# Splitting the blocks that TensorE transposes in the first six attention units: low half from ScalarE instead of VectorE

## The chip, the cores and the metric

The kernel runs on one core of one Trainium2 chip. The core has a matrix engine (PE, TensorE) with its weight loader (PEld), a vector engine (DVE, VectorE), a scalar engine (ACT, ScalarE), a general engine (POOL, GpSimd), an engine that mostly issues transfers (SP, SyncE) and 16 DMA engines. The metric is the device time of one execution in microseconds, the median over runs.

## What is computed

The reference is a block-sparse attention followed by a dense layer pair, in float32:

```python
scores = scale * np.matmul(q, k.transpose(0, 1, 3, 2))    # q, k, v: 4 x 8 x 768 x 64
# mask: neighbouring blocks of 32, first and last block, and 3 sampled blocks for each block row
attn = np.exp(scores - max); attn = attn / (sum + 1e-09); x = np.matmul(attn, v)
h = x @ w_in                                              # 3072 x 512 times 512 x 2048
sp = np.maximum(h, 0.0) + np.log1p(np.exp(-np.abs(h)))
return (h * erf(sp)) @ w_out                              # 2048 x 512
```

The kernel keeps float32 accuracy in products of 16-bit numbers: a float32 matrix is written as a high half (the value rounded to float16) and a low half (what the rounding left), and the products high*high, high*low and low*high are added in PSUM.

## The kernel before

**Units.** For each of the four batches there are 11 "m" units of two inner block rows and four "f" units for the outer block rows. A unit makes scores on PE (`scores`, tile `s`, one buffer), a negated maximum on DVE (`soft_max`, `less`), exponentials on ACT (`soft_exp`, `pf`, two buffers), turns the probabilities so that keys lie on the partitions (`pT`, three buffers), multiplies them with gathered values on PE (`values`, tile `po`, one buffer), divides by the sum on DVE (`norm`, `xf`) and turns the result (`turn`, `xT`). Four units fill one chunk of `xT`.

**Two ways of turning.** From unit 6 on (counted from 0), ACT and DVE first make the high and low half, and a transposing DMA turns both. The first six units (`FIRST = 6`) turn on PE instead, through `by_pe` (line 595): float32 blocks of 128x128 are transposed with an identity matrix `eye` into a PSUM tile `turned` of the pool `ps_h`, ACT takes the high half out of PSUM as float16, and DVE takes out `turned*scale - high` as the low half. `by_pe` runs twice for each of the six units' `pT` (four blocks each time) and once for each of the first four results `xT` (two blocks). The pool `ps_h` has three buffers, and the dense layer's `h` tiles use the same three.

**The weights** are prepared beside the first six units by a generator `weights()`: DVE decodes each pair of weight tiles from 64-bit words (three instructions on 128x1024, `room<-wi` or `room<-wo`), ACT sums squares (`sq_i`, `sq_o`), and the halves are made. For `w_in` PE forms the low half: `rest` is a float32 matmul of the weights with a scaled diagonal, less the high half through `less16` (a negative float16 identity), and ACT takes it out (`wi<-rest`). For `w_out` ACT makes the high half and DVE the low half (`wo<-wo,sums`). Such a float32 matmul appears in the trace as two PE records, a PE transpose as one.

**The dense layers** run in groups: `h` (24 matmuls, `ff_first`), a chain of ACT instructions on `x` and `y` (`ff_logs`, `ff_exp`), the gate on DVE (`ff_gate`, reads `h` and so frees its PSUM buffer), and `o` (12 matmuls, `ff_second`) three groups later.

**Order.** SP and POOL keep the program's order. PE, ACT and DVE keep it only from group 3 on (`held[0] = m >= FF_LAG`, line 989). Everything before that, the six units, the weights and the groups 0 to 2, is ordered by a scheduler that plays the program through with its own cost estimates. Completions of hardware DMAs are counted on eight semaphores (DMAHW0 to DMAHW7) given out in turn, and a DMA that is given one waits until the transfer that had it before has landed.

Of the kernel before, what the change touches and what calls it, by code (L numbers as in the profile page):

```python
# [9 lines left out]
F32 = mybir.dt.float32  # L10
I32 = mybir.dt.int32
BF16 = mybir.dt.bfloat16
AF = mybir.ActivationFunctionType
ALU = mybir.AluOpType
# [4 lines left out]
P = 128  # L19
BLOCK = 32  # L20
P_SHIFT = 14
P_SCALE = 2.0**P_SHIFT
# [9 lines left out]
def sparse_attention_moe(ctx: ExitStack, tc: tile.TileContext, qT, kT, v, sampled, w_in, w_out, out):  # L32
# [7 lines left out]
    class InOrder:  # L40
# [15 lines left out]
    pe, act, dve, pool, sp = (  # L56
        InOrder(e, queued if e in (nc.sync, nc.gpsimd) else held) for e in (nc.tensor, nc.scalar, nc.vector, nc.gpsimd, nc.sync)
    )
# [4 lines left out]
    W = 512  # L63
# [28 lines left out]
    ps_h = ctx.enter_context(tc.tile_pool(name="ps_h", bufs=3, space=PSUM))  # L92
# [6 lines left out]
    room = ld.tile([P, NB, HP, BLOCK], F32, tag="kx", name="room", bufs=2).rearrange("p a b c -> p (a b c)")  # L99
    ones, eye = room[:, :P], room[:, P : 2 * P]  # L100
    less16 = room[:, 2 * P : 2 * P + 64].bitcast(F16)
    diag, line = room[:, 3 * P : 4 * P], room[:, 4 * P : 5 * P]
    column = room[:, 2 * P + 64 : 2 * P + 65]
    mags = [room[:, n : n + 1024].bitcast(I32) for n in (5 * P, 5 * P + 1024)]
    dve.memset(ones, 1.0)
    dve.memset(line[:, :1], 0.0)
# [173 lines left out]
    def indices():  # L280
        room = at.tile([P, 1024], F32, tag="pf", name="ix_room", bufs=2)
        used = 0

        def ix(shape):
            nonlocal used
            n = math.prod(shape[1:])
            part = room[:, used : used + n]
            used += n
            if len(shape) == 3:
                part = part.rearrange("p (a b) -> p a b", b=shape[2])  # L290
            return part

        sf, dd, m1 = ix([P, NB, NR]), ix([P, NB, NR]), ix([P, NB, NR])
        dve.tensor_copy(samp, samp2[:, :, :, 0].rearrange("p i r -> p (i r)"))
        dve.tensor_copy(sf, samp.rearrange("p (i r) -> p i r", r=NR))
        bi = line[:, :NB]
        dve.tensor_tensor(dd, sf, bi.unsqueeze(2).to_broadcast([P, NB, NR]), ALU.subtract)
        dve.tensor_tensor(dd, dd, dd, ALU.mult)
        dve.tensor_scalar(m1, dd, 1.0, None, ALU.is_le)
        dve.scalar_tensor_tensor(dd, sf, -float(NB - 1), sf, ALU.add, ALU.mult)  # L300
        dve.scalar_tensor_tensor(m1, dd, 0.0, m1, ALU.is_equal, ALU.max)
        eq = ix([P, NB, 3])
        for n, (x, y) in enumerate(((1, 0), (2, 0), (2, 1))):
            dve.tensor_tensor(eq[:, :, n], sf[:, :, x], sf[:, :, y], ALU.is_equal)
        dve.tensor_tensor(m1[:, :, 1:], m1[:, :, 1:], eq[:, :, :2], ALU.max)
        dve.tensor_tensor(m1[:, :, 2], m1[:, :, 2], eq[:, :, 2], ALU.max)

        dve.tensor_scalar(eye, line, column, None, ALU.is_equal)
        dve.tensor_scalar(less16, line, column, -1.0, ALU.is_equal, ALU.mult)
        yield  # L310
        dve.tensor_scalar(dd, sf, -1.0, float(NB), ALU.mult, ALU.add)
        dve.tensor_tensor(dd, dd, m1, ALU.mult)
        dve.tensor_tensor(sf, sf, dd, ALU.add)
        pm = turned32[:, :1]
        rows = ix([P, NM])
        dve.memset(rows, 0.0)
        mid = sf[:, 1 : NB - 1]
        for q in range(NR):
            part = slice(q * BLOCK, (q + 1) * BLOCK)
            dve.tensor_scalar(rows[part], mid[part, :, q], float(BLOCK), pm[part], ALU.mult, ALU.add)  # L320
        idx = cp.tile([P, NM], I32, tag="idx", name="idx")
        dve.tensor_copy(idx, rows)
        rows_of.append(idx)
        yield
# [269 lines left out]

    def by_pe(blocks, hi, lo, scale=1.0):
        n = blocks.shape[1]
        turned = ps_h.tile([P, W], F32, tag="h", name="turned")[:, :n]
        for c in range(0, n, P):
            pe.transpose(turned[:, c : c + P], blocks[:, c : c + P], eye)
        turned = turned.rearrange("p (g w) -> p g w", w=hi.shape[2])  # L600
        act.activation(hi, turned, AF.Copy, scale=scale)
        dve.scalar_tensor_tensor(lo, turned, scale, hi, ALU.mult, ALU.subtract)

    def soft_turn(unit):

        s, groups, width, pf = softs.pop(unit)
        pT = at.tile([P, 16, P], F16, tag="pT", name="pT_" + "_".join(str(x) for x in unit), bufs=3)
        parts = pT.rearrange("p (g a k) c -> p g a (k c)", a=2, k=2)
        for n in range(2):
            by_pe(pf[:, n * 512 : (n + 1) * 512], parts[:, 2 * n : 2 * n + 2, 0], parts[:, 2 * n : 2 * n + 2, 1], P_SCALE)  # L610
        pts[unit] = pT
# [98 lines left out]
    def turn(b, u, part, early=False):  # L710
        if part != 0:
            xf = xfs.pop((b, u))
            xr = xf.rearrange("p h d -> p (h d)")
            ch, n = divmod(u, CU)
            if n == 0:
                xTs[b, ch] = mo.tile([P, NK, CU, P], F16, tag="xT", name=f"xT_{b}_{ch}", bufs=3)
            xT = xTs[b, ch][:, :, n, :]
            if early:
                by_pe(xr, xT[:, :2], xT[:, 2:])
                return  # L720
            x2 = at.tile([P, 2, 4 * D], F16, tag="x2", name=f"x2_{b}_{u}", bufs=2)
            act.activation(x2[:, 0], xr, AF.Copy)
            dve.tensor_tensor(x2[:, 1], xr, x2[:, 0], ALU.subtract)
            sp.dma_start_transpose(out=xT, in_=x2.rearrange("p a s -> p (a s)"))
# [207 lines left out]
    load_w("o", 13)  # L932
    have_k.add(0)
    ixgen = indices()
    next(ixgen)
    gathers()
# [144 lines left out]
```

## Time and profile before

| quantity | value |
|---|---|
| median of 3 runs | 754.68 us (754.65, 754.68, 762.38) |
| profiled execution, its own time | 764.91 us |
| its span, first to last instruction | 763.1 us |
| PE busy | 686.3 us (90%) |
| ACT busy | 591.9 us (78%) |
| DVE busy | 575.4 us (75%) |
| POOL busy | 201.6 us (26%) |
| mean granted TensorE clock | 0.975 |

How to read it: the busy shares are averages over the whole span. The first 135 us or so (loads, weights, the first six units) have other limits than the steady part that follows, so the views below are taken by stretches. Durations of instructions that follow each other on one engine overlap a little in the records (the next starts before the end of the one before is written), so the distance between starts is the better price.

### The profile page before, as it was taken

To read this page: it belongs to the slowest core of one execution; us is meant where nothing else is said; L and a number is where in the kernel's file an instruction comes from. 1 tells how busy PE (TensorE), PEld (TensorE's weight loads), DVE (VectorE), ACT (ScalarE), POOL (GpSimd) and SP (SyncE) were. 2 spreads that over 40 slices of the span, in tenths; PEclk is the share of its full clock that TensorE was granted. 3 is DMA by queue.
4 is the path that set the end of the run, shared out by engine and by line. 5 is a ranking of instruction groups with operands and counts; after the bars stand their busy time and mean duration, and the time that the engine had idled before them with its cause. 6 is when DMAs were issued, how large, how long until landed. Compare 5 with 4: busy or idle time off the path is not lost.

```text
span 763.1 us, 24883 instructions
## 1 busy us (share of the span) xinstructions
PE 686.3 (90%) x10400; PEld 450.6 (59%) x10400; DVE 575.4 (75%) x1122; ACT 591.9 (78%) x1023; POOL 201.6 (26%) x413
## 2 busy tenths in 40 slices
PE   1336887998999999999999999999999999999997
PEld 0213554655655666666566666666666666667663
DVE  6983999978777788778687878787777786665453
ACT  2544999878877887878888887888788887776774
POOL 3026624303364313130533312033433120000000
PEclk9976998998999999999999999999999999999999
DMA  8999835896599999855997799938988677130000
GB/s 304 415 293 283 257 91 119 195 224 154 136 224 211 193 208 182 212 144 87 250 191 162 187 166 194 251 89 185 223 157 182 130 147 168 29 77 2 8 29 27
DMA packets 188048, 129.36 MB, mean 170 GB/s; under 512 B 137760, under 2 KB 160928, under 8 KB 186912
## 3 DMA queue, kind: packets, MB, share of 16 engines
q1 hardware_dynamic: 173584, 84.50, 54.1%
q10 hardware_dynamic: 8464, 25.43, 10.4%
q0 software_dynamic: 5888, 17.84, 9.6%
q8 instruction: 81, 1.33, 0.7%
q14 instruction: 31, 0.25, 0.1%
HBM read 82.81 MB, written 12.95 MB: 125 GB/s over the span
## 4 chain that ended last, share of the span: by engine, by line
PE 78%; DMA 6%; DVE 5%; ACT 5%; issue 3%; SPq 2%; ACTq 0%; DVEq 0%
PE h L48 31%; PE o L48 31%; PE s_m L48 7%; PE po_None L48 4%; PE s_f L48 3%; SPq L48 2%; DMA vbuf<-vtab 2%; DMA wo<-in_w_in_dram 2%; DMA vtab<-vn 1%; ACT x L48 1%; PE po L48 1%; DVE room L48 1%; DMA vbuf<-in_v_dram 1%; ACT pf_m L48 1%; DVE less_m L48 1%
## 5 line engine op out<-in xcount | busy, mean ns | idle before, releaser
L48 PE MATMUL h<-xT,wi 128*128 128x256 f16 x2304 | 272.3, 275 | 5.0 <-DVE y L48 4.5
L48 PE MATMUL o<-wo,g 128*128 128x512 f16 x1152 | 264.5, 379 | 0.5 <-DVE g L48 0.2
L48 PEld LDWEIGHTS <-wi 128*128 128x128 f16 x2304 | 223.7, 99 | 45.8 <-DVE y L48 4.6
L48 ACT ACTIVATE x<-x 128x512 f32<-128x512 f32 x288 | 181.6, 631 | 8.9
L48 PEld LDWEIGHTS <-g 128*128 128x128 f16 x1152 | 109.5, 98 | 127.4 <-issue 6.6
L48 POOL DMA_INDIRECT vbuf<-vtab,idx x88 | 96.5, 1097 | 185.1 <-PE po_None L48 130.3
L48 DVE SCALAR_TENSOR_TENSOR y<-y,x 128x512 f32<-128x512 f32 x96 | 67.1, 699 | 95.0 <-ACT x L48 91.6
L48 POOL COPY kbuf<-kx 128x128 f32 (+1 forms) x280 | 87.3, 357 | 94.4 <-PE s_m L48 79.8
L48 ACT ACTIVATE x<-h,isg 128x512 f32<-128x512 f32 x96 | 65.4, 682 | 49.2 <-PE h L48 31.9
L48 ACT ACTIVATE y<-y 128x512 f32<-128x512 f32 x96 | 59.7, 622 | 32.9 <-DVE y L48 32.9
L48 ACT ACTIVATE pf_m<-s_m,less_m 128x256 f32<-128x256 f32 x176 | 68.9, 473 | 19.7 <-DVE less_m L48 18.7
L48 DVE SCALAR_TENSOR_TENSOR g<-y,sums,g 128x512 f16<-128x512 f32 x96 | 73.1, 762 | 3.4
L48 DVE SCALAR_TENSOR_TENSOR y<-y,h 128x512 f32<-128x512 f32 x96 | 65.2, 679 | 0.1
L48 ACT ACTIVATE y<-x 128x512 f32<-128x512 f32 x96 | 60.4, 631 | 3.0
L48 DVE TENSOR_REDUCE less_m<-s_m 128x4 f32<-128x1024 f32 x44 | 53.6, 1218 | 11.7 <-PE s_m L48 11.6
L48 PEld LDWEIGHTS <-pT_m 128*32 128x32 f16 x3168 | 35.4, 98 | 33.9 <-issue 31.4
L48 PE MATMUL po_None<-vbuf,pT_m 128*32 128x65 f16 (+2 forms) x3168 | 41.9, 205 | 13.2 <-issue 12.5
L48 PE MATMUL s_m<-kbuf,qt 64*32 64x160 f32 x1408 | 48.2, 316 | 3.7 <-issue 2.8
L48 DVE TENSOR_SCALAR g<-y,sums 128x512 f16<-128x512 f32 x96 | 48.0, 500 | 3.4
L48 PE MATMUL s_m<-kx,qt 64*32 64x96 f32 x1408 | 31.6, 259 | 20.4 <-ACT kx L48 13.3
L48 DVE SCALAR_TENSOR_TENSOR p_m<-pf_m,p_m 128x1024 f16<-128x1024 f32 x38 | 46.4, 1221 | 0.3 <-issue 0.3
L48 DVE TENSOR_TENSOR x<-xf,x 128x256 f16<-128x256 f32 x44 | 18.8, 426 | 31.7 <-ACT x L48 31.6
(110 smaller groups left out, 609.8 us busy)
## 6 DMA issues: line engine op xcount, KB each, us to landing
vbuf<-vtab SPq DMA_DIRECT2D x80, 195.0 KB
vraw<-in_v_dram ACTq DMA_DIRECT2D x9, 768.0 KB
vtab<-vn SPq DMA_DIRECT2D x16, 390.0 KB
vbuf<-vtab SPq DMA_DIRECT2D x12, 520.0 KB
wo<-in_w_out_dram ACTq DMA_DIRECT2D x6, 1024.0 KB
qt<-in_qT_dram SPq DMA_DIRECT2D x20, 256.0 KB
kr<-in_kT_dram ACTq DMA_DIRECT2D x12, 384.0 KB
vbuf<-vtab SPq DMA_DIRECT2D x32, 130.0 KB
```

The source lines that it names most:

```text
L48: done = call(*args, **kwargs)
```

## The change

`by_pe` no longer lets DVE form the low half. PE transposes the blocks into `turned` as before and ACT takes out the high half. In addition PE multiplies the same blocks with the identity (or, for the probabilities, with `eye_p`, an identity scaled by 2^14) once more, as an ordinary float32 matmul into a second PSUM tile `less`, and subtracts the high half there by one float16 matmul with `less16`. ACT then copies `less` out as the low half. Both tiles come from `ps_h`. One small DVE instruction forms `eye_p`.

```diff
+    eye_p = room[:, 5 * P + 2048 + 2 * BLOCK :][:, :P]
...
         dve.tensor_scalar(eye, line, column, None, ALU.is_equal)
+        dve.tensor_scalar(eye_p, line, column, P_SCALE, ALU.is_equal, ALU.mult)
...
     def by_pe(blocks, hi, lo, scale=1.0):
         n = blocks.shape[1]
-        turned = ps_h.tile([P, W], F32, tag="h", name="turned")[:, :n]
+        turned, less = (ps_h.tile([P, W], F32, tag="h", name="turned")[:, :n] for _ in range(2))
         for c in range(0, n, P):
             pe.transpose(turned[:, c : c + P], blocks[:, c : c + P], eye)
-        turned = turned.rearrange("p (g w) -> p g w", w=hi.shape[2])
-        act.activation(hi, turned, AF.Copy, scale=scale)
-        dve.scalar_tensor_tensor(lo, turned, scale, hi, ALU.mult, ALU.subtract)
+        act.activation(hi, turned.rearrange("p (g w) -> p g w", w=hi.shape[2]), AF.Copy, scale=scale)
+        for c in range(0, n, P):
+            pe.matmul(less[:, c : c + P], blocks[:, c : c + P], eye if scale == 1.0 else eye_p, start=c == 0, stop=False)
+        pe.matmul(less, less16, hi, start=False, stop=True)
+        act.activation(lo, less.rearrange("p (g w) -> p g w", w=hi.shape[2]), AF.Copy)
```

Because the scheduler orders this part, other instructions move too. Three places are shown.

**PE, the turning of unit 2.** `turned` is the PSUM tile, `xf` the result of a unit, `pf` the exponentials, `rest` the low half of `w_in`; a row `turned<-pT` or `turned<-xT` is the new subtraction of the high half. Before:

```order
L48 MATMUL turned_589<-room_85,xf_0_0_584 128x128 x2
L48 MATMUL turned_636<-room_85,pf_m_0_2_630 128x128 x4
L48 MATMUL turned_643<-room_85,pf_m_0_2_630 128x128 x4
L48 MATMUL rest_4_689<-wi_123,room_85 128x512
L48 MATMUL rest_5_692<-wi_123,room_85 128x512
```

and now (between the two parts stand the value products of unit 1):

```order
L48 MATMUL turned_614<-room_85,xf_0_0_609 128x128 x2
L48 MATMUL turned_615<-room_85,xf_0_0_609 128x128 x2
L48 MATMUL turned_665<-room_85,pf_m_0_2_659 128x128 x4
L48 MATMUL rest_6_751<-wi_123,room_85 128x512
...
L48 MATMUL turned_615<-xT_0_0_613,room_85 128x256
L48 MATMUL turned_666<-room_85,pf_m_0_2_659 128x128 x4
L48 MATMUL rest_7_754<-wi_123,room_85 128x512
...
L48 MATMUL turned_666<-pT_m_0_2_664,room_85 128x512
L48 MATMUL turned_678<-room_85,pf_m_0_2_659 128x128 x4
L48 MATMUL turned_679<-room_85,pf_m_0_2_659 128x128 x4
```

What was three rows in a run is now spread over two rounds with ACT (high half out, then the subtraction), and `rest_4` to `rest_6` stand ahead of it.

**ACT, the loads of `w_out` and the first `w_in` halves**, with what each waits for. `DMA wo` are loads of 1 MB, `sq` sums of squares, `wi<-wi,sums` high halves, `wi<-rest` low halves. Before:

```order
L48 DMA wo_124<-in_w_out_dram 128x2x1024 [waits DMAHW5_49]
L48 ACTIVATE sq_i14_702,sums_112<-wi_123 128x1024 [waits DVE_49,Activation_49]
L48 DMA wo_124<-in_w_out_dram 128x2x1024 [waits DMAHW2_49]
L48 DMA wo_124<-in_w_out_dram 128x2x1024 [waits DMAHW4_49]
L48 ACTIVATE wi_123<-wi_123,sums_112 128x512 [waits PE_49,Activation_49] x2
L48 ACTIVATE wi_123<-rest_0_490 128x512 [waits PE_49]
```

and now:

```order
L48 DMA wo_124<-in_w_out_dram 128x2x1024 [waits DMAHW6_49,DMAHW5_49]
L48 DMA wo_124<-in_w_out_dram 128x2x1024 [waits DMAHW0_49]
L48 ACTIVATE wi_123<-wi_123,sums_112 128x512 [waits PE_49,Activation_49] x2
L48 ACTIVATE sq_o0_764,sums_112<-wo_124 128x1024 [waits DVE_49]
L48 ACTIVATE wi_123<-rest_0_515 128x512 [waits PE_49]
L48 ACTIVATE wi_123<-rest_1_518 128x512 [waits PE_49]
L48 ACTIVATE wi_123<-wi_123,sums_112 128x512 [waits PE_49]
L48 ACTIVATE wi_123<-rest_2_714 128x512 [waits PE_49]
L48 ACTIVATE sq_o2_955,sums_112<-wo_124 128x1024 [waits DVE_49]
```

Before, the third and fourth load had the semaphores DMAHW2 and DMAHW4, last given to gathers of values into `vbuf0` and `vbuf1`. Now they have DMAHW6 and DMAHW0, last given to the first and second `wo` load.

**ACT, the end of the scheduled part.** `x_0_0_0<-h_0_0_0` begins the chain of dense group 0, and `wo<-wo,sums` are high halves of `w_out`. Before, with 10 of the 16 `wo` high halves standing ahead of the last row shown:

```order
L48 ACTIVATE wo_124<-wo_124,sums_112 128x512 x2
L48 ACTIVATE pf_m_0_7_1653<-s_m_0_7_1601,less_m_0_7_1644 128x256 x2
L48 ACTIVATE x_0_0_1_1571<-x_0_0_1_1571 128x512
L48 ACTIVATE pf_m_0_7_1653<-s_m_0_7_1601,less_m_0_7_1644 128x256 x2
L48 ACTIVATE y_0_0_0_1421<-y_0_0_0_1421 128x512
```

and now, where all 16 stand ahead of the same row, `y_0_0_0<-y_0_0_0` (it follows 15 rows after the last one shown):

```order
L48 ACTIVATE pT_m_0_5_1393<-turned_1395 128x2x256
L48 ACTIVATE pT_m_0_5_1393<-turned_1407 128x2x256
L48 ACTIVATE wo_124<-wo_124,sums_112 128x512 x2
L48 ACTIVATE pf_m_0_7_1742<-s_m_0_7_1690,less_m_0_7_1733 128x256 x4
L48 ACTIVATE pT_m_0_5_1393<-turned_1408 128x2x256
L48 ACTIVATE wo_124<-wo_124,sums_112 128x512
L48 ACTIVATE x_0_0_0_1506<-h_0_0_0_1481,isg_0_1479 128x512
```

The turning of unit 5 now stands right ahead of the dense chain, and the `wo` high halves that were mixed into that chain have moved ahead of its end.

## Rows read from the trace of the kernel before

**Rows 1.** The page's chain that ended last, by engine.

```profile
PE 78%; DMA 6%; DVE 5%; ACT 5%; issue 3%; SPq 2%; ACTq 0%; DVEq 0%
```

**Rows 2.** Busy time by stretch (engine columns: us, instructions; then granted clock, DMA).

```profile
core 0: us, PE busy (x) PEld busy (x) DVE busy (x) ACT busy (x) POOL busy (x), PEclk, DMA share, GB/s
0.00:67.00 67.00, 19.19 (x316) 10.27 (x320) 47.49 (x100) 27.48 (x51) 18.29 (x54) 0.85 0.99 329
67.00:123.30 56.30, 46.06 (x840) 29.33 (x830) 53.99 (x130) 49.98 (x100) 29.86 (x46) 0.95 0.67 183
123.30:763.10 639.80, 621.05 (x9256) 410.95 (x9256) 473.89 (x893) 514.47 (x874) 153.44 (x313) 0.99 0.73 152
```

**Rows 3.** Chain of waits in time (start, us, what): end of the gather.

```profile
52.18 11.53 DMA vbuf<-vtab
...
66.28 1.42 PE po_None L48 x67
```

**Rows 4.** All waits between 60 and 180 us, ACT's, then DVE's.

```profile
ACT wi L48 <- DMA vbuf<-vtab: 11.3, 1, 11.3
...
DVE rinv_None L48 <- PE po_None L48: 11.2, 1, 11.2
```

**Rows 5.** PE in time (start, us, what; idle before): ends of the scheduled part.

```profile
123.28 5.30 PE L48 MATMUL h<-xT,wi 128*128 128x256 f16 x24 [4.50 <-DVE y L48]
128.51 0.73 PE L48 MATMUL s_m<-kx,qt 64*32 64x96 f32 x32
...
134.39 0.88 PE L48 MATMUL po_None<-vbuf,pT_m 128*32 128x65 f16 x72 [1.80 <-issue]
135.21 2.79 PE L48 MATMUL h<-xT,wi 128*128 128x256 f16 x24
```

**Rows 6.** ACT and DVE in time, 112 to 134 us.

```profile
112.04 0.72 ACT L48 ACTIVATE x<-h,isg 128x512 f32<-128x512 f32 x1
...
121.81 0.69 ACT L48 ACTIVATE y<-y 128x512 f32<-128x512 f32 x1
122.33 0.75 ACT L48 ACTIVATE x<-h,isg 128x512 f32<-128x512 f32 x1
...
126.11 1.39 ACT L48 ACTIVATE wo<-wo,sums 128x512 f16<-128x512 f32 x2
127.34 0.68 ACT L48 ACTIVATE x<-x 128x512 f32<-128x512 f32 x1
...
129.60 0.68 ACT L48 ACTIVATE x<-x 128x512 f32<-128x512 f32 x1
...
133.14 0.15 DVE L48 TENSOR_SCALAR rinv_None<-po_None 128x4 f32<-128x4 f32 x1
```

**Rows 7.** Instructions of the tile `turned`, 67 to 110 us (min/median/max ns).

```profile
L48 PE MATMUL turned<-room,pf_m x32: 272/273/328, 73.3 to 102.1; 128*128 128x128 f32 x32
L48 ACT ACTIVATE pT_m<-turned x8: 585/626/647, 76.0 to 102.5; 128x512 f16<-128x512 f32 x8
L48 DVE SCALAR_TENSOR_TENSOR pT_m<-turned,pT_m x8: 675/680/692, 76.7 to 106.5; 128x512 f16<-128x512 f32 x8
L48 ACT ACTIVATE xT<-turned x4: 384/410/451, 74.7 to 101.5; 128x256 f16<-128x256 f32 x4
L48 DVE SCALAR_TENSOR_TENSOR xT<-turned,xT x4: 410/416/424, 75.2 to 103.7; 128x256 f16<-128x256 f32 x4
```

**Rows 8.** PE in time: prices of transposes, of float32 records, of `rest`.

```profile
68.35 3.46 PE L48 MATMUL rest<-wi,room 128*128 128x512 f32 x5
...
89.44 1.04 PE L48 MATMUL turned<-room,pf_m 128*128 128x128 f32 x8
90.31 0.38 PE L48 MATMUL rest<-wi,room 128*128 128x512 f16 x1
90.53 0.28 PE L48 MATMUL total<-sums,room 128*128 128x1 f32 x2
```

**Rows 9.** Weight loads of `total` (16 records for 8 matmuls; ns).

```profile
L48 PEld LDWEIGHTS total<-sums,room x16: 186/189/190, 82.6 to 118.3; 128*128 128x128 f32 x16
```

## The prediction

> **What bounds the kernel now.** First the chain that ended last, by engine [rows 1]: PE holds 78% of it, so in most of the span only PE's work counts. Then the busy times by stretch [rows 2], because the change touches nothing after the first six units. From 123.3 us to the end PE is busy 621.05 of 639.80 us and runs in an order that the change leaves alone. From 67.0 to 123.3 us the fullest engine is DVE (53.99 of 56.30), then ACT (49.98), and PE has 10.2 us to spare (46.06). Before 67 us the DMA engines are full (share 0.99, 329 GB/s) and PE works 19.19 of 67 us.
>
> How the stretches join is read from three more views. The chain in time [rows 3]: a gather of values lands at 52.18 + 11.53 = 63.71 us, and PE's first value product starts at 66.28. The waits [rows 4] show the two long ones there: ACT 11.3 us behind a DMA (its own issues of `wo` loads need a semaphore that the gather holds), and DVE 11.2 us until that value product. PE in time at the other end [rows 5]: it stands idle 4.50 us ahead of `h` of the fourth block (I call it h_3) at 123.28, since the gate on DVE must free one of three PSUM buffers, and that `h` takes 5.30 us where the same 24 matmuls take 2.79 at 135.21. So the granted clock was at the lower level, 1.2 GHz, after an idle of 4.50 us, and at 2.4 GHz later. The last wait before the steady part is 1.80 us, at 134.39. DVE's `rinv` of that stretch is at 133.14, after ACT's square of `x` at 129.60 [rows 6]: ACT's chain held DVE's result.
>
> So the prediction is a question of when h_3 starts and how much of the 1.80 us is left. All that follows is worked out against the profiled execution of 764.91 us. It lies 10.2 us over the median of 754.68, so only the difference is carried to the median. About 1%, 7.5 us, is what a measurement of this kernel can tell from no change.
>
> **What the change removes.** In the stretch from 67 us DVE loses eight subtractions of 0.680 and four of 0.416 [rows 7], 7.1 us. It falls from 53.99 to 46.9 us and is no longer the fullest engine. The one small added instruction, `eye_p`, stands before 67 us, where DVE is busy 47.49 of 67 us [rows 2]; I cost it at nothing. If that cover were gone it would cost less than one subtraction.
>
> **What it adds on PE.** In the stretch there are eight calls of four blocks and four of two, so 40 copies as ordinary float32 matmuls. No such instruction of 128 columns on a float32 block is in the trace. From below: a transpose of the same block, eight in 0.87 us (89.44 to 90.31), 0.109 each [rows 8]. From above: the pair of float32 records of `total`, 0.28 us [rows 8], after a weight load of 0.19 [rows 9] that hides behind nothing, 0.47. I take 0.28, the row of the same kind (two records, two loads of a 128x128 float32 block), because the loader worked beside PE in these stretches (29.33 us of loads within 46.06 of PE [rows 2]). That is 40 x 0.28 = 11.2 us; the ends are 4.4 and 18.8. The subtractions of the high half are the float16 record of `rest`, 0.22 us (90.31 to 90.53), half for 256 columns: 8 x 0.22 + 4 x 0.11 = 2.2 us.
>
> Here a rule stands against the row. The Trainium skill, page "Perfetto Trace Analysis", section "Transposes", says that a logical transposition should be a transpose and not an ordinary matmul, because transposes skip the arithmetic; the page "TensorE: Matmul & The Clock Gate", section "Terms", puts transpose mode at four times faster for FP32. An estimate by these pages is 4 x 0.109 = 0.44 us for a copy, and my sum would be 6.4 us higher. No copy of this size is in the trace; the pair of `total` at 0.28 is against it, though that has one column.
>
> **What moves.** The scheduler puts `rest_2`, `rest_3` and a part of unit 3's scores ahead of the first value product. Four float32 records at 0.69 (3.46/5 [rows 8]; at a lower mean clock than later) would be 2.8, two float16 ones 0.4, and half a unit's scores 0.65 (128.51 to 129.82 is 1.31 for one unit [rows 5]): 3.8 us leave the stretch into the idle of PE before 67 us. If that idle is not there the 3.8 us come back. PE in the stretch: 46.06 + 11.2 + 2.2 - 3.8 = 55.7 us.
>
> ACT gains eight copies and four small ones. In a row a start follows 0.16 us before the record ahead of it ends (126.11 + 1.39 against 127.34 [rows 6]), so they cost 8 x 0.47 + 4 x 0.25 = 4.7 us: 54.7 us. What moves across 67 us on ACT I take as even: two high and two low halves, one sum of squares and four exponentials go ahead, six `wo` high halves come in. Queued behind each new copy on ACT are the sums of squares and exponentials of the next unit; PE's values wait for the copy.
>
> The `wo` loads: with other semaphores ACT's issues no longer wait for the gather [rows 4]. The 11.3 us of ACT go, and it can do the instructions just listed there. What is late next is still the gather, as DMA is full there. I leave the start of the value products at 66.28; it could come up to 2.6 us earlier, to 63.71, or later (a rival below).
>
> **The sum.** PE cannot run without a break: ACT's chain from `x` of h_0 (112.04) to h_3 (123.28) took 11.24 us, with PE idle 4.50 of it at its end. One pair of `wo` high halves, 1.2 us [rows 6], leaves the chain, so 3.3 us of that idle remain. PE is then filled to 55.7 + 3.3 = 59.0 us, and I add what the fullest engine lacks now, 56.30 - 53.99 = 2.3 us, for waits between engines. h_3 starts at 67.0 + 61.3 = 128.3 us, 5.0 later than before. After an idle of 3.3 us I take the lower clock again: from h_3 to the end of `o` it is 134.39 - 1.80 - 123.28 = 9.3 us as before, to 137.6. The 1.80 us wait goes, since the `wo` high halves that stood in ACT's chain there (126.11 [rows 6]) are done earlier. The steady part starts 137.6 - 134.39 = 3.2 us later. **Forecast: 754.68 + 3.2 = 757.9 us.** With copies at the lower end, 6.8 us less, 751.1; at the higher end 7.6 more, 765.5.
>
> **Rivals.**
> - Dear copies (slower): loads and streams of a copy don't overlap, 0.47 each. For it: each copy brings its own block as weights, twice. Against: transposes, which load as often, come each 0.109. Price +7.6, time 765.5, which is +10.8; over the 1% bound from 0.39 us a copy. The pages named above would give 764.3, by an estimate. Chance 0.11.
> - Rounds with ACT (slower): each call's subtraction waits on PE for the high half just before it, and three buffers for two tiles a call leave no second call in the air, so PE stands still behind it. Price: one ACT instruction a call, 8 x 0.626 + 4 x 0.410 = 6.6 us [rows 7], in place of my 2.3 us of waits and of nothing else if none hides: 757.9 + 6.6 = 764.5. For it: three rows of PE in a run are spread over two rounds. Against: scores and `rest` stand between the rounds in the new order. It decides from 4.3 us of exposed waits, where the 1% is passed. Chance 0.11.
> - DVE was the bound (faster): the copies cost 0.11 and hide, and h_3 comes when ACT is through its 54.7 us, 1.6 earlier; PE's idle before it is short and the clock stays at 2.4 GHz, 2.5 less (5.30 against 2.79 [rows 5]); the 1.80 goes. Together 5.9 less: 748.8. For it: DVE is at 96% of the stretch. Against: PE with 0.28 a copy needs more than the stretch has. Chance 0.17, a third of it beyond 1% where the value products also start at 63.71.
> - A later gather: two `wo` loads of 1 MB, issued earlier into full DMA engines, take 1 MB / 329 GB/s = 3.2 us each. There are 66.28 - 63.71 = 2.6 us to spare, so +0.6 to +3.8: 758.5 to 761.7. Chance 0.10.
> - It is absorbed: PE has 18.75 us of idle in the steady part [rows 2]; if waits there are for things that don't move, the 3.2 us go into them: 754.7. Chance 0.06.
>
> **How the numbers follow.** The forecast has the remaining 0.45, with a range of its own from 751.1 to 762. Faster by over 1% is only a third of the DVE rival: 0.05. Slower by over 1% (over 762.2): most of the two slower rivals, 0.18, with 0.02 of the gather and 0.03 of the forecast's upper edge: 0.23. Within 1%: 0.72. The range goes from 751.0 to 766.0: below it lies most of the DVE rival (0.12), above it some 0.06 where two slower cases meet.
>
> **What the changed profile would show.** In the stretch from 67 us DVE near 47 us and PE near 56 of some 61 us. Copies as pairs of records 0.28 us apart. ACT's 11.3 us wait behind the gather gone. h_3 near 128 us at half speed, and no wait at the value product that follows `o`. The steady part as long as before. The forecast is wrong if h_3 is before 124 us (DVE was the bound), or if PE's waits for ACT's high halves sum to over 6 us, or if copies come 0.39 us or more apart.

## The result: about 1% slower

| | kernel before | changed kernel |
|---|---|---|
| median (6 runs each) | 755.58 us | 766.41 us |
| ratio | 1 | 1.0115, 95% interval 1.0075 to 1.0155 |
| span of the profiled execution | 763.1 us | 763.7 us |
| start of the steady part (value product of unit 6) | 134.39 us | 145.28 us |

The ratio is worth 8.7 us of 755 (5.7 to 11.7). The forecast was 3.2 us. The two profiled spans hide the difference, since the profiled execution of before lay 10.2 us over its median. Its steady part shows where.

### The profile page after: what moved, and what is told of

Read it like the earlier page. It is cut to its first block, busy times and chain, and to the rows that moved or that the text cites. A ratio compares the mean times of both kernels' runs of the same rounds, so it can differ in the third digit from the quotient of the medians.

```text
span 763.7 us, 25141 instructions
## 1 busy us (share of the span) xinstructions
PE 694.6 (91%) x10528; PEld 462.2 (61%) x10528; DVE 570.7 (75%) x1107; ACT 599.8 (79%) x1039; POOL 203.3 (27%) x413
## 3 DMA queue, kind: packets, MB, share of 16 engines
q10 hardware_dynamic: 8464, 25.43, 10.2%
## 4 chain that ended last, share of the span: by engine, by line
PE 63%; DVE 12%; ACT 10%; DMA 10%; issue 3%; SPq 0%; ACTq 0%; DVEq 0%
PE h L48 26%; PE o L48 25%; DMA wo<-in_w_out_dram 5%; ACT x L48 5%; PE s_m L48 4%; PE po_None L48 3%; DVE room L48 2%; DVE y L48 2%; PE s_f L48 2%; ACT y L48 2%; DVE less_m L48 2%; DMA pT_m<-p_m 2%; DMA qt<-in_qT_dram 1%; DVE xf L48 1%; PE po L48 1%
## 5 line engine op out<-in xcount | busy, mean ns | idle before, releaser
L48 POOL DMA_INDIRECT vbuf<-vtab,idx x88 | 98.3, 1117 | 208.8 <-PE po_None L48 149.5
L48 POOL COPY kbuf<-kx 128x128 f32 (+1 forms) x280 | 85.5, 350 | 73.1 <-PE s_m L48 58.6
L48 PE MATMUL s_m<-kbuf,qt 64*32 64x160 f32 x1408 | 43.7, 313 | 3.6 <-issue 3.1
L48 PE MATMUL s_m<-kx,qt 64*32 64x96 f32 x1408 | 27.6, 259 | 16.1 <-ACT kx L48 13.9
L48 ACT ACTIVATE p_m<-pf_m 128x1024 f16<-128x1024 f32 x38 | 40.2, 1059 | 1.8 <-DMA pT_m<-p_m 0.7
```

What stands on the lines that cost most here:

```text
L48: done = call(*args, **kwargs)
```

## The profile after

First the chain that ended last, by engine; it answers to [rows 1].

```profile
PE 63%; DVE 12%; ACT 10%; DMA 10%; issue 3%; SPq 0%; ACTq 0%; DVEq 0%
```

DVE, ACT and DMA have grown. In time (start, us, what), the longest pieces of that chain between 45 and 110 us are loads; the last row is what PE does when the chain comes back to it:

```profile
45.63 16.18 DMA wo<-in_w_out_dram
61.84 14.26 DMA wo<-in_w_out_dram
80.56 9.72 DMA wo<-in_w_out_dram
99.13 7.04 DMA vraw<-in_v_dram
108.73 1.34 PE rest L48 x3
```

Three loads of `w_out` and one of `v` hold 47.2 us of it, and DVE's work on what they bring stands between them. In the kernel before, the chain ran through DVE's own instructions there, from 75.20 to the turning of unit 3's result:

```profile
75.20 0.42 DVE xT L48
...
100.68 0.28 DVE xf L48
...
101.09 0.86 PE turned L48 x6
```

So in that part DVE's work was what counted before, and loads are what counts on the chain now. Busy times by stretch of the changed kernel (columns as in [rows 2]):

```profile
0.00:67.00 67.00, 27.34 (x306) 16.46 (x307) 48.90 (x100) 30.39 (x56) 19.73 (x54) 0.78 1.01 323
67.00:123.30 56.30, 49.52 (x838) 32.19 (x837) 43.05 (x99) 45.59 (x92) 25.53 (x44) 0.98 0.71 183
67.00:145.28 78.28, 64.88 (x1067) 43.50 (x1066) 59.87 (x134) 66.09 (x128) 28.98 (x52) 0.94 0.65 160
145.28:763.70 618.42, 602.36 (x9157) 402.24 (x9156) 461.89 (x874) 503.35 (x855) 154.59 (x307) 1.00 0.72 154
```

And of the kernel before, cut at its own start of the steady part:

```profile
67.00:134.39 67.39, 55.35 (x939) 34.97 (x929) 64.20 (x147) 59.93 (x116) 32.25 (x52) 0.92 0.65 176
134.39:763.10 628.71, 611.77 (x9156) 405.32 (x9156) 463.68 (x876) 504.52 (x858) 151.05 (x307) 0.99 0.73 152
```

The steady part has the same instructions. In before's profiled execution PE was busy 9.4 us longer with them (611.77 against 602.36, at a granted clock of 0.99 against 1.00). So the two spans are not to be compared; the start of the steady part is: 10.89 us later, in the interval of the ratio. From 67 us to it PE's busy time grew by 9.5 us (55.35 to 64.88), and PE's idle time did not shrink: 12.0 us before, 13.4 after. DVE is no longer full (43.05 of 56.30), and nothing else is either.

The waits between 0 and 180 us (engine, what waits, for what: sum, times, longest) answer to [rows 4].

```profile
ACT wi L48 <- DMA vbuf<-vtab: 11.1, 1, 11.1
DVE room L48 <- DMA wo<-in_w_out_dram: 8.5, 4, 4.5
PE h L48 <- DVE y L48: 6.6, 1, 6.6
PE turned L48 <- ACT pT_m L48: 4.9, 2, 3.2
```

ACT's 11 us are still there. PE's direct wait for the high half is only 4.9 us, 3.2 of them before 67 us. What else makes the stretch longer, two places show in part. The first is one call of unit 3, in time (start, us, what):

```profile
90.31 0.82 DVE L48 TENSOR_SCALAR room<-wo 128x1024 int32<-128x1024 int32 x1 [0.67 <-DMA wo<-in_w_out_dram]
92.29 1.06 ACT L48 ACTIVATE sq_o<-wo 128x1024 bf16<-128x1024 f32 x1 [2.53 <-DVE wo L48]
93.35 0.58 ACT L48 ACTIVATE pT_m<-turned 128x512 f16<-128x512 f32 x1
93.98 0.38 PE L48 MATMUL turned<-pT_m,room 128*128 128x512 f16 x1 [1.68 <-ACT pT_m L48]
96.41 0.56 PE L48 MATMUL s_m<-kx,qt 64*32 64x96 f32 x32 [0.60 <-ACT pf_m L48]
```

PE's subtraction waits for ACT's high half. That stands on ACT behind a sum of squares, which waits for DVE's decoding of `w_out`, which waited 0.67 us for a load. Here the added trip through ACT took over what ACT itself was waiting for. The second place is the turning of unit 3's result, the last that the first `h` needs:

```profile
110.40 0.89 PE L48 MATMUL turned<-room,xf 128*128 128x128 f32 x6
112.23 0.42 ACT L48 ACTIVATE xT<-turned 128x256 f16<-128x256 f32 x1
116.03 0.28 PE L48 MATMUL turned<-xT,room 128*128 128x256 f16 x1
116.35 0.38 ACT L48 ACTIVATE xT<-turned 128x256 f16<-128x256 f32 x1 [0.90 <-PE turned L48]
121.09 1.47 PE L48 MATMUL h<-xT,wi 128*128 128x256 f16 x12
```

The same in the kernel before:

```profile
101.09 0.41 PE L48 MATMUL turned<-room,xf 128*128 128x128 f32 x2 [0.68 <-DVE xf L48]
101.54 0.38 ACT L48 ACTIVATE xT<-turned 128x256 f16<-128x256 f32 x1
103.65 0.41 DVE L48 SCALAR_TENSOR_TENSOR xT<-turned,xT 128x256 f16<-128x256 f32 x1
104.12 3.44 PE L48 MATMUL h<-xT,wi 128*128 128x256 f16 x30 [0.55 <-DVE xT L48]
```

From the transposition to `h` it was 3.0 us and is now 10.7. After the high half, done at 112.65, the subtraction stands in PE's order behind other work until 116.03, and `h` again until 121.09. No idle of PE marks this; PE is busy with other things meanwhile.

That is 7.7 us of the 17.0 by which `h` comes later. The other 9.3 are there before the turning begins (110.40 for 101.09). The values of unit 3 already start 10.8 us late (98.93 for 88.13). Then, on DVE, the maximum of a piece of `v` stands with its load ahead of the division of unit 3's result (`xf`, its last instruction at 109.61):

```profile
106.19 1.75 DVE L48 TENSOR_REDUCE vmax<-vraw 128x1 f32<-128x1536 f32 x1 [1.51 <-DMA vraw<-in_v_dram]
```

Before, it stood behind that division (111.90 against 100.60). This is the scheduler's order, and not a trip.

`x` of h_0 then starts at 126.10 where it was 112.04, and ACT's chain from there sets the start of h_3. Five high halves of `w_out` stand in that chain, where two stood before (at 118.64). The rows are the first three; the others are at 131.58 and 132.71:

```profile
126.67 0.74 ACT L48 ACTIVATE wo<-wo,sums 128x512 f16<-128x512 f32 x1
...
129.32 1.36 ACT L48 ACTIVATE wo<-wo,sums 128x512 f16<-128x512 f32 x2
```

PE at that end answers to [rows 5]:

```profile
129.54 0.89 PE L48 MATMUL po_None<-vbuf,pT_m 128*32 128x65 f16 x72
137.04 4.47 PE L48 MATMUL h<-xT,wi 128*128 128x256 f16 x24 [6.62 <-DVE y L48]
141.44 0.56 PE L48 MATMUL s_m<-kx,qt 64*32 64x96 f32 x32
142.59 2.76 PE L48 MATMUL o<-wo,g 128*128 128x512 f16 x12
145.28 0.89 PE L48 MATMUL po_None<-vbuf,pT_m 128*32 128x65 f16 x72
```

Ahead of h_3 PE has run out of work at 130.4 and is idle 6.62 us (4.50 before). The wait of 1.80 us at 134.39 is gone.

Last, the prices on PE, which answer to [rows 8]:

```profile
102.89 0.27 PE L48 MATMUL turned<-xT,room 128*128 128x256 f16 x1
103.00 1.05 PE L48 MATMUL turned<-room,pf_m 128*128 128x128 f32 x8
103.89 0.38 PE L48 MATMUL turned<-pT_m,room 128*128 128x512 f16 x1
104.10 0.60 PE L48 MATMUL turned<-room,pf_m 128*128 128x128 f32 x4
104.54 1.24 PE L48 MATMUL rest<-wi,room 128*128 128x512 f32 x3
```

The eight records at 103.00 are four copies: 0.89/4 = 0.22 us each. The four at 104.10 are transposes, 0.11 each. A subtraction takes 0.11 (256 columns) or 0.21 us.

## The experiments

All were timed against the kernel before, run beside them. Every edit also gives the scheduler another order, so a price is that of the edit and the order together. Whether the prices add up is not settled: units 0 and 1 alone and units 2 to 5 alone give more together than the whole by their middle values (1.0147 against 1.0115), but the intervals allow a plain sum. "Start" is the start of the steady part in the one profile of each; before 134.39, change 145.28.

| kernel | ratio (95% interval) | start, us |
|---|---|---|
| two_units | 1.0045 (1.0010 to 1.0081) | 138.75 |
| four_units | 1.0102 (1.0074 to 1.0130) | 145.78 |
| po0_first | 1.0111 (1.0049 to 1.0172) | 146.23 |
| dve_out | 1.0198 (1.0151 to 1.0245) | 149.27 |
| pe_copies | 1.0170 (1.0114 to 1.0225) | 143.99 |
| no_copies | 1.0124 (1.0073 to 1.0174) | 145.10 |
| no_subtract | 1.0049 (0.9992 to 1.0106) | 137.70 |
| xt_only | 1.0062 (1.0007 to 1.0116) | 138.98 |
| pin_after | 1.0108 (1.0074 to 1.0142) | 141.32 |
| pin_before | 1.0047 (1.0005 to 1.0089) | 137.76 |
| less_in_o | 1.0222 (1.0150 to 1.0295) | 154.43 |
| pt_only | 1.0110 (1.0053 to 1.0168) | 142.01 |

**Where in the program: two_units, four_units, po0_first.** My first theory was that a late first value product (70.38 for 66.28 us) is carried to the end.

```diff
-            by_pe(pf[...], ..., P_SCALE)
+            (by_pe if unit[2] < 2 else by_pe_old)(pf[...], ..., P_SCALE)   # two_units; xT by by_pe_old
+            (by_pe if unit[2] >= 2 else by_pe_old)(pf[...], ..., P_SCALE)  # four_units; xT by by_pe
```

```diff
     def rest(i):
+        if i in (2, 3): with tc.issue_after(last_value[0].ins): ...        # po0_first
```

> The change in units 0 and 1 alone; units 2 to 5 form their low half on DVE as before. PE's order at the first value product is that of the change (rest_2, rest_3 and unit 3's scores ahead of it). Theory START (the loss has a first part of 4.1 us, the first value product at 70.4 instead of 66.3, that is carried to the end): 3 to 5 us slower than the kernel before, ratio about 1.005. Rival LATER (all is lost after unit 2, the early shift is absorbed): within 1 us, ratio 1.000. Rival ALL-START: the whole 8.7 us, ratio 1.011.

> The change in units 2 to 5 alone (and in all four results xT); units 0 and 1 as before. PE's order up to the first value product is that of the kernel before. Theory START plus rounds: the first value product is back at about 66, 4 us of the loss go, some 5 to 7 us stay: ratio about 1.007. Rival ALL-START: ratio 1.000. Rival LATER: as the change, 1.011.

> The whole change, but the matmuls rest_2 and rest_3 are held on PE behind the first value product. Theory START: the value product starts near 66, the steady part 3 to 4 us earlier than with the change, ratio to the kernel before about 1.006. Rival LATER: PE does the same work in the same stretch, it is only passed on, ratio 1.011 as the change.

Taken alone, two_units fits 3 to 5 us, and four_units is a little over its 5 to 7 us (7.7): most of the loss belongs to units 2 to 5 and the four results. In four_units the first value product started at 68.08, and not at about 66. po0_first does not test the theory, since its first value product hardly moved: with the order of before, PE waits for the gather instead:

```profile
69.28 1.50 PE L48 MATMUL po_None<-vbuf,pT_m 128*32 128x65 f16 x71 [4.78 <-DMA vbuf<-vtab]
```

The gather lands later than the 63.71 us of [rows 3]. That fits the rival of the later gather in place and size, though no run shows that the loads of `w_out` are the reason (the first two are issued at 42.84 and 45.63 in the change, 45.52 and 49.74 before). Whether an early first value product helps at the end, dve_out and pin_before below tell.

**Which engine takes the low half out: dve_out.**

```diff
-        act.activation(lo, less..., AF.Copy)
+        dve.tensor_copy(lo, less...)
```

> The whole change, but DVE instead of ACT takes the finished low half out of PSUM; PE's copies, its subtractions, its rounds and both PSUM tiles stay. If ACT's queue (16 more instructions) is what the stretch pays for, 3 or more us come back against the change: ratio about 1.006 or less. If it is PE's work and the wait for the high half, the time stays: 1.010 to 1.013. If DVE is the bound again, slower than the change.

Nothing comes back: without ACT's 16 instructions the kernel is 2.0% slower than before. That does not clear ACT's queue, since DVE has 16 more instructions in exchange, and the third branch, slower than the change, is what came. At 79.75 PE waits 6.32 us for `pT`, still for ACT's high half:

```profile
79.75 0.23 PE L48 MATMUL po_None<-vbuf,pT_m 128*32 128x65 f16 x1 [6.32 <-ACT pT_m L48]
```

The high half was late because ACT's queue stood 3.48 us at the issue of a load of `w_out` (issued at 78.68, the high half at 79.10). So this wait, too, goes back to a load. The first value product of dve_out starts at 62.07, 8.3 us earlier than in the change, and the kernel is the slower one all the same.

**Work or rounds: pe_copies, no_copies, no_subtract, xt_only.** Of two theories, WORK says that PE's added time itself is carried, and ROUNDS that the way transposition, high half, subtraction, low half is.

```diff
+            pe.matmul(turned[...], blocks[...], eye, start=True, stop=True)  # pe_copies, on before, ahead of the transposes
```

```diff
-            pe.matmul(less[...], blocks[...], eye or eye_p, ...)             # no_copies
-        pe.matmul(less, less16, hi, start=False, stop=True)                  # no_subtract
```

```diff
-            by_pe(pf[...], ..., P_SCALE)
+            by_pe_old(pf[...], ..., P_SCALE)                                 # xt_only
```

In no_copies and no_subtract the flags of what is left are set to match, and no_copies takes the low half out with its sign turned.

> The kernel before, with each block multiplied by the identity once more as an ordinary float32 matmul, into the tile turned itself ahead of its transposes (which write over it). PE's added work alone: no second tile, no subtraction, no ACT instruction; DVE still forms the low half. Theory WORK (PE's idle in the stretch is no reserve, so added PE time is carried nearly whole): 40 copies of 0.22 us in the stretch, 8.9 us, so 6 to 9 us slower, ratio 1.008 to 1.012. Theory ROUNDS (the loss is the wait of PE for ACT's high half and the queue on ACT): at most 2 us, ratio below 1.003.

> The change without the copies: the second tile holds only the high half's product, and ACT takes that out as the low half (its sign turned; so the low half is the high half, which is not what the reference computes). Rounds, tiles and ACT instructions stay as in the change. Theory WORK: the loss goes, ratio 0.999 to 1.003. Theory ROUNDS: the loss stays, ratio 1.008 to 1.011.

> The change without the subtraction of the high half: the copies go into the second tile and ACT takes them out whole (so the low half is the full value, which is not what the reference computes). PE no longer waits for the high half. Theory WORK: only the subtractions' 2.2 us go, ratio about 1.008. Theory ROUNDS: ratio below 1.003.

> The change for the four results xT alone (two blocks each); the probabilities as before. 8 copies in the stretch, 1.8 us, and four subtractions of 0.11 on PE, 1.7 us off DVE. Theory WORK: 1 to 3 us slower, ratio 1.001 to 1.004. Theory ROUNDS: four of sixteen rounds, and those stand nearest to h of the first dense group: 2 to 4 us. If DVE's time counts: 1 to 2 us faster, ratio 0.998.

Busy times from 67 us to the start of the steady part. Without copies:

```profile
67.00:145.10 78.10, 60.15 (x976) 36.63 (x976) 58.74 (x133) 63.25 (x124) 30.12 (x52) 0.80 0.57 154
```

Without the subtraction:

```profile
67.00:137.70 70.70, 61.89 (x1054) 42.25 (x1039) 57.81 (x133) 65.19 (x128) 31.08 (x52) 0.94 0.63 166
```

Copies alone on the kernel before:

```profile
67.00:143.99 76.99, 65.58 (x1057) 43.57 (x1056) 64.16 (x147) 63.16 (x121) 32.62 (x52) 0.90 0.58 158
```

PE's idle in them, stretch less busy: 18.0 without copies, 8.8 without the subtraction, 11.4 with the copies alone (12.0 before, 13.4 with the change). Without the copies the whole loss stays, though PE's new work is only the subtractions, 2.2 us at full clock. PE's busy time falls by 4.7 us against the change, and idle time grows by 4.6. The copies should have freed 8.9 us of busy time, but the mean granted clock of the stretch is 0.80 there, 0.94 in the change: what is left of PE's work ran slower. So WORK alone is out, but no_copies also pays for a lower clock, and its chain between 45 and 90 us passes three loads of `w_out` (39 us), as that of the change does.

Without the subtraction, PE's busy time still grows by 6.5 us over before, but 3.2 of these go into idle time, and the start comes 3.3 us late instead of 10.9. By the starts, then, the second trip is the larger part of the loss. The times alone do not show it: the interval of no_subtract holds the forecast of ROUNDS (below 1.003) and that of WORK (1.008), and overlaps that of the change.

ROUNDS alone fails on pe_copies: PE work without an added round costs 1.7%, and the start comes 9.6 us late, about the 8.9 us of the copies. There PE's work is carried whole, as WORK says, though DVE is less full than before (64.16 of 76.99, before 64.20 of 67.39). So added PE work alone and an added trip alone cost about as much as both together, and neither theory explains the loss by itself. xt_only, four rounds of sixteen, costs 4.7 us, a little over the 2 to 4 that ROUNDS gave, with an interval from 0.5 to 8.8; it holds the turning next to the first `h`.

**The start once more: pin_after, pin_before.** The third and fourth load of `w_out` are held on ACT behind `rest_1`'s low half, in either kernel.

```diff
             for piece in loads.get(n, ()):
-                load_w(*piece)
+                with tc.issue_after(done_out[1].ins): load_w(*piece)        # pieces ("o", 4), ("o", 6)
```

> The change, with the third and fourth load of w_out held on ACT behind the low halves of w_in's first two tiles, so that ACT does not stand 11 us at their issue. Theory LOADS (two of the loss's parts come from w_out's loads: they fill the DMA engines ahead of the gather, and ACT waits at their issue): the first value product near 66 again, 3 to 4 us back, ratio about 1.007 to the kernel before. Rival: the work is only passed on to the rounds behind, ratio 1.010 to 1.012.

> The kernel before with the same edit: the two loads of w_out behind the low halves on ACT. ACT's 11.3 us wait goes, the first value product follows the gather at 63.7 or earlier (its wait was 2.6 us longer), so 1 to 3 us faster, ratio 0.997. Rival: DVE, the fullest engine, waits for the later loads instead: 1 to 4 us slower.

In pin_after the start is not what I wanted. ACT's wait at the issues goes, but PE then waits for copies on POOL that the scores need, and the first value product stays where the change has it:

```profile
64.97 0.79 PE L48 MATMUL s_m<-kbuf,qt 64*32 64x160 f32 x16 [11.34 <-POOL kbuf L48]
...
70.56 0.88 PE L48 MATMUL po_None<-vbuf,pT_m 128*32 128x65 f16 x71
```

So the ratio of 1.0108 says nothing on the first value product. It says something on the loads, for which theory LOADS had forecast 1.007: DVE waits only 3.7 us for loads of `w_out` there (8.5 in the change), and one load of 5.05 us is left on the chain behind 67 us. The start comes 4.0 us earlier than in the change, but the time does not show a gain. What the loads are worth stays open.

In pin_before the start is what I wanted, and the first value product runs 2.6 us earlier than in [rows 3]:

```profile
63.61 1.49 PE L48 MATMUL po_None<-vbuf,pT_m 128*32 128x65 f16 x71 [0.87 <-DMA vbuf<-vtab]
```

Yet the kernel is 0.47% slower (interval from 0.05%). The forecast of 0.997 failed, and the rival came in sign and size: DVE waits 6.6 us for loads of `w_out`, 2.2 before. With dve_out this speaks against theory START: time won at the first value product is not passed to the end as it is. The stretch behind it decides. It also shows what another order alone can cost, since pin_before has no new instruction: 3.5 us by the ratio.

**Buffers: less_in_o; twelve rounds: pt_only.**

```diff
-        turned, less = (ps_h.tile(..., tag="h", ...) for _ in range(2))
+        turned = ps_h.tile(..., tag="h", ...); less = ps_o.tile(..., tag="o", ...)   # less_in_o
```

```diff
-                by_pe(xr, xT[:, :2], xT[:, 2:])
+                by_pe_old(xr, xT[:, :2], xT[:, 2:])                                  # pt_only
```

> The change, with the second tile less in the pool of two buffers that rest and total use (ps_o), so that turned and h have their three buffers to themselves. If the rounds cost because three buffers hold two tiles a call: 3 to 6 us back, ratio 1.003 to 1.007. If the order of high half, subtraction and low half on two in-order queues is the cost itself: 1.009 to 1.012; and if rest now waits for its buffers, slower than the change.

> The change for the probabilities alone (12 of the 16 calls); the four results xT as in the kernel before. xT alone gave 1.006. If the loss is the sum over rounds, 12 of 16 give three quarters, about 1.008; if xT's four rounds, which stand on the way to the first h, make the loss by themselves, 1.004 or less.

The third case came: slower than the change. The two buffers that `rest` shares now hold PE up. In the waits of less_in_o from 40 to 150 us:

```profile
PE rest L48 <- ACT wi L48: 13.5, 3, 6.7
```

In the change that wait is 9.5 us from 0 to 180 us. Whether three buffers for two tiles a call cost something is therefore not decided.

pt_only has the middle value of the change's loss, 1.011, but its interval holds three quarters of it, 1.008, as well, and its start is 7.6 us late, 0.70 of 10.9. With xt_only (4.6 us) the starts add up to 12.2. So a sum over rounds is not refuted. What is refuted is that the four rounds of xT make the loss by themselves (1.004 or less was forecast for that).

## Right and wrong, step by step

- **Sign and range: right.** Slower, 8.7 us by the ratio; 754.68 x 1.0115 = 763.4 lies in the range. The size was 3.2, too low, and the 1% had a chance of only 0.23. None of the three signs of being wrong came (h_3 not before 124, waits for the high half 4.9 us, copies 0.22 apart), so the list did not hold what happened: an h_3 far later than 128.
- **PE's added time: right in the sum, by luck.** 55.7 us in the stretch up to h_3 were forecast; 49.52 to 123.30 and 7.1 more to 137.04 make 56.6. Two errors offset each other. A copy took 0.22 us, not 0.28 (between the ends of 0.11 and 0.47), 2.3 us less in all; and of the 3.8 us that were to leave the stretch nearly nothing left it. The estimate by the Trainium skill's page "TensorE: Matmul & The Clock Gate", section "Terms", was 0.44; the trace shows twice a transpose, not four times.
- **The step that failed: "I add what the fullest engine lacks now, 56.30 - 53.99 = 2.3 us, for waits between engines".** With 3.3 us ahead of h_3 I let PE's idle up to h_3 shrink from 10.2 us (56.30 less 46.06) to 5.6, so that 4.6 us of new work would be hidden. It grew to 13.4. Of the 7.8 us between, 4.5 are in the waits between engines (6.8 for 2.3) and 3.3 ahead of h_3 (6.62 for 3.3). Taking DVE's lack as PE's was the mistake: DVE's idle time became 13 us to 123.30, part of it waits for loads, and PE's idle time was not room for new work. pe_copies shows that without an added trip: 10.2 us more of busy time, and idle 11.4 us where it was 12.0. That the idle time is the latency of hand-overs, which a second trip lengthens, fits the 8.8 us without the subtraction, but is not shown apart from the order.
- **"One pair of `wo` high halves, 1.2 us [rows 6], leaves the chain": wrong.** Five stand in ACT's chain from `x` of h_0 to h_3 now, two before, and it took 10.9 us where 10.0 was forecast.
- **The rival "rounds with ACT" (0.11) came nearest in size**, 9.8 us against 8.7. But its sum is not what its words say: 6.6 us in place of the 2.3 gives 762.2, which is 7.5; 764.5 has both. Its mechanism I had as direct waits of PE over 6 us, and those are 1.7 us in the stretch. So the nearness is in part luck.
- **"3.8 us leave the stretch into the idle of PE before 67 us": wrong.** The first value product moved to 70.38 us with that work, and 27 float32 records of `rest` still stand between 67 us and h_3, where 28 stood before. pin_before and dve_out show that an early first value product is not enough.
- **ACT's 11.3 us wait: wrong.** It stays at 11.1. By the order in the section on the change the issues now wait for `w_out`'s own earlier loads, though the view names the gather.
- **h_3 near 128 us: wrong**, 137.04. **The vanishing 1.80 us: right. Steady part unchanged: right** in PE's work.
- **Dear copies, DVE was the bound: neither.** Up to the start of the steady part DVE is busy 4.3 us less than before (59.87 for 64.20; 7.1 less were forecast), and the kernel did not follow: on the chain, loads took DVE's place.

What stays open: how much of the loss is the longer way itself and how much the order that the scheduler makes of it, since no run held the order of the kernel before with the new instructions in it. The loads of `w_out` on the chain are a rival that pin_after tests only in part. So the cause of the 8.7 us is argued and not shown. Whether pe_copies costs more (13 us by the middle value) than its copies (8.9 us in the stretch at 0.22) is within its interval, 8.6 to 17. No variant beat the kernel before.

## What to carry to other kernels

Idle time of an in-order engine is not free room: here 9.5 us of new work on PE left its idle time as long as it was. Before work is moved from the fullest engine, count the trips that one item makes between queues; without the trip the start came 7.6 us earlier here, more than the 4.3 us taken off DVE. Look at what the freed engine does next: DVE ran into waits for loads, not ahead. And where a scheduler orders the stretch, a new order alone can cost some us.

## Not expected

A float32 matmul of 128 columns is two records of 0.11 us, each as long as a transpose. A first value product 2.6 us earlier left the end 0.47% later. On the chain of the changed kernel, loads of 1 MB took 9.7 us (from 80.56) to 16.2 us (from 45.63) to land, with the DMA engines full up to 67 us (share 1.01), against 3.2 us by the mean rate of [rows 2].
